# Sliding-window attention feeding a cosine MLP: where q, k and v are loaded and turned within a stage, and three normalisations on another engine

## The chip, the cores and the metric

The kernel runs on one core of a Trainium2 chip. The metric is device time in microseconds (us); the time before is 332.21 us, the median of three runs (330.58 to 332.81). Everything below is read from one profiled execution and its trace.

A core has five engines, each with its own queue that is worked off in order. TensorE (PE) multiplies; its weight loads are shown as PEld. VectorE (DVE) and ScalarE (ACT) read TensorE's results out of PSUM and work on them. GpSimd (POOL) cannot read PSUM; here it normalises, copies, and issues the loads of q, k and v, which are converted from 32 to 16 bit on their way. SyncE (SP) issues the DMAs that transpose, and the stores. SP's and POOL's transfers have a queue each (q1 and q0 on the page), and the same 16 DMA engines serve both.

## The reference, cut to what matters

```python
# q, k, v: (8, 8, 576, 64)   batch, heads, positions, head size
scores = (q @ k^T) / 8
keep   = 0 <= pos_q - pos_k < 64            # causal window of 64
attn   = softmax(where(keep, scores, -1e9)) @ v
x = attn.transpose(0, 2, 1, 3).reshape(8 * 576, 8 * 64)     # 4608 x 512
h = x @ w_in                                # 512 x 2048
out = (h * cos(h)) @ w_out                  # 2048 x 512
```

A block of 64 queries needs its own 64 keys and the 64 before them, so a *unit* is 64 queries by 128 keys of one batch, one pair of heads (128 rows of q, two heads) and one block j of 0 to 8.

## The kernel before, in words

**Stages.** The 4608 rows of x are worked off in nine tiles of 512 rows, mt = 0 to 8 (L485). A stage is one tile through the MLP: 64 matmuls with w_in (L359, into `h_ps`), with sine on ScalarE (L504) and the product on VectorE (L507) behind them, and then 64 matmuls with w_out (L519, into `out_ps`). Eight blocks make a tile and nine make a batch, so tile mt needs the last blocks of batch mt - 1 and the first ones of batch mt; of batch mt it needs blocks 0 to 5 in tile 2, 0 to 4 in tile 3, and 0 to 3, 0 to 2, 0 and 1 after that.

**Attention inside a stage.** Beside stage mt the attention of batch mt + 1 is computed, in groups of three or four units (`groups`, cut up by `CUTS`, L29). Each group passes through `g_scores` (PE, L263), `g_max` (DVE, L286), `g_exp` (ACT, L297), `g_inv` (DVE, L304), `g_norm` (POOL, L311; tile `w`), and `g_trans`: a DMA transpose that SP issues (L323; tile `wT`). In the first stage some groups (`direct`) are transposed on PE instead. `values` (PE, L338) multiplies wT by v into `o_ps`; `put_x` (L112) copies that into `xT`, the next tile's operand. PE works in the order in which it was given its work: the scores of the groups stand between the out_ps matmuls, from the first of them on, and `values` stands at the end of the stage, ahead of the next stage's h_ps matmuls. A stage has ten groups; the first four to seven of them (six in stages 1 and 2, four in stages 3 to 6) hold the blocks that the next tile needs.

**Loads and turns.** For a batch b from 2 on, `load_chunk` (L146) loads q and k in five chunks each, `load_v` (L152) loads v in five, all from POOL's queue. `turn` (L213) transposes a whole q or k in two DMAs from SP's queue, a main one (16 blocks of 128 by 128) and a small one; the results are `qX` and `kX`. `spread_q` (DVE, L221) copies qX into the block layout `qB` that the scores use; `spread_v` (POOL, two copies at L112) writes the copies of v that are shifted by 64 rows.

**The plan.** `at(time, fn, ...)` puts a step into a list with a time in units of about one us of a stage (a stage has T = 32 units), and `pump(time)`, called after each of the stage's steps, emits all steps that are due. So the planned times settle the order in each engine's queue, and nothing else: no instruction waits for a time. For batch b, t0 = 32 (b - 1) is the start of stage b - 1, in which its scores are computed (from t0 + 14.6 units on).

Before, in a stage from 2 to 5, POOL's queue holds, after the last normalisation of a stage: k (5 loads), q (5), then v (5), then the next stage's first five or six normalisations, `spread_v`, and the rest. SP's queue holds two stores, kX, qX, then the ten `wT`. k and q that are loaded in a stage are those of the batch whose scores come one stage later; v is that of the scores at hand.

The tiles k, q, kX, qX, and v have two buffers each. A DMA's issue waits, in its engine's queue, for its data, for its buffer, and for the DMA eight before it on the same engine to have landed.

Of the kernel before, what the change touches and what calls it, by code (L numbers as in the profile page):

```python
# [24 lines left out]
NC = 5  # L25
# [15 lines left out]
T = 2 * Q  # L41
# [17 lines left out]
def kernel(  # L59
# [182 lines left out]
    n_first = len(groups)  # L242
# [143 lines left out]
    def at(time, fn, *args):  # L386
        plan.append((time, len(plan), fn, args))
# [9 lines left out]
    n = n_first  # L397
    for t in range(B - 1):
        last = max(i for i, units in enumerate(groups) if units[0][0] == t + 1)
        time = T * t + Q - 1.4  # L400
        for i in range(last + 1 - n):
            time += PACE * len(groups[n - 1]) if i else 0
            at(time - 1.05 * (i % 2) * (t == 0), g_scores, n, i % 3)
            lags = LAGS[:2] + tuple(T * t + T - 0.79 - time + 0.01 * s for s in range(3)) if n == last and t else LAGS
            for lag, fn in zip(lags, (g_max, g_exp, g_inv, g_norm)):
                at(time + lag, fn, n)
            at(time + (4.6 if n in direct else lags[-1]), g_trans, n)
            if n in direct:
                at(time + 4.9, g_put, n)
            ready.update({unit: time + (5.9 if n in direct else 8.5) for unit in groups[n]})  # L410
            n += 1

    for b in range(1, B):
        t0 = T * (b - 1)
        if b == 1:
            for p in range(PAIRS):
                for lag, fn in ((0, tr_q), (0.01, tr_k), (0.02, put_q), (0.03, put_k)):
                    at(7 + 1.8 * p + lag, fn, b, p)
        else:
            for i, name in enumerate(("k", "q")):  # L420
                for c in range(NC):
                    at(t0 - T + 0.4 + 0.9 * (c + NC * i) if b > 2 else 4 + 0.5 * c if i else 27.5 + 0.9 * c, load_chunk, name, b, c)
                for c, (lo, hi) in enumerate(((0, 4), (4, 5))):
                    at((t0 + 3 if b == 2 and not i else t0 - T + 13.3 + 1.2 * i + (b == 2) * 9) + 0.6 * c, turn, name, b, lo, hi)
            for c, (lo, hi) in enumerate(((0, 4), (4, 5))):
                for h in range(2):
                    at(t0 + 4.2 + h + 2 * c, spread_q, b, h, lo, hi)
            for c in range(5):
                at(t0 + 9.4 + 0.9 * c, load_v, b, c)
            for half in range(2):  # L430
                at(t0 + 24.2 + 0.1 * half, spread_v, b, half)
    for half in range(2):
# [3 lines left out]
    for mt in range(1, n_mt):  # L436
        for p in range(PAIRS):
            time = max(ready[b, p - p % 2 + i // TU, j] for i in range(2 * TU) for b, j in (divmod(mt * TU + i % TU, NU),))
            time = max(time, 25.5) if mt == 1 else T * mt - (8.01 if mt == n_mt - 1 else 1.01)
# [27 lines left out]
    turn, turn_h = iter(range(100)), iter(range(100))  # L467
# [91 lines left out]
```

## Time and profile before

| What | Value |
|---|---|
| median of three runs | 332.21 us (330.58 to 332.81) |
| profiled execution, its own time | 332.94 us |
| its span | 331.2 us |
| mean granted TensorE clock | 0.968 |
| PE busy | 304.9 us, 92% of the span |
| ACT, DVE, POOL busy | 71%, 67%, 60% |
| DMA: q0 (POOL's loads), q1 (SP's) | 74.7% and 41.0% of 16 engines' span |
| h_ps matmuls, L359 | 576, 133.3 us |
| out_ps matmuls, L519 | 560, 132.8 us |
| normalisations on POOL, L311 | 78, 73.4 us, 956 ns in the mean |

Times are from the span's start. An entry such as `[3.36 <-DMA wT<-w]` behind a row is the idle time of the engine before it and what ended it. "SPq" rows are SP's issues of DMAs: their length is the time that the issue took SP's queue, not that of the transfer. "Landing" is the time from an issue's start to the moment at which the data are there.

The first scores of stages 1 to 6 start at 82.82, 119.88, 152.36, 184.48, 223.09 and 254.05 us. The later text calls these moments s1 to s6.

### The profile page before, as it was taken

To read this page: it belongs to the slowest core of one execution; us is meant where nothing else is said; L and a number is where in the kernel's file an instruction comes from. 1 tells how busy PE (TensorE), PEld (TensorE's weight loads), DVE (VectorE), ACT (ScalarE), POOL (GpSimd) and SP (SyncE) were. 2 spreads that over 40 slices of the span, in tenths; PEclk is the share of its full clock that TensorE was granted. 3 is DMA by queue.
4 is the path that set the end of the run, shared out by engine and by line. 5 is a ranking of instruction groups with operands and counts; after the bars stand their busy time and mean duration, and the time that the engine had idled before them with its cause. 6 is when DMAs were issued, how large, how long until landed. Compare 5 with 4: busy or idle time off the path is not lost.

```text
span 331.2 us, 7510 instructions
## 1 busy us (share of the span) xinstructions
PE 304.9 (92%) x2452; PEld 154.2 (47%) x2452; DVE 222.0 (67%) x847; ACT 236.0 (71%) x785; POOL 197.2 (60%) x218
## 2 busy tenths in 40 slices
PE   3989999589996999899999993999999999999996
PEld 2654554234543455445544551445544554454443
DVE  5896877449862887588749871598679857533811
ACT  3987799436992789778977895369977997314700
POOL 9995166999489627994699559843970690000000
PEclk9979999979996999999999998799999999999999
DMA  7999993999999999599979997999697435011012
GB/s 98 174 210 208 198 166 78 129 127 218 173 143 100 208 156 127 91 202 161 149 110 125 201 168 110 121 225 152 120 112 169 50 64 162 0 65 64 0 55 74
DMA packets 165960, 43.56 MB, mean 132 GB/s; under 512 B 155104, under 2 KB 161440, under 8 KB 165920
## 3 DMA queue, kind: packets, MB, share of 16 engines
q0 software_dynamic: 99632, 18.36, 74.7%
q1 hardware_dynamic: 66144, 24.52, 41.0%
q8 instruction: 19, 0.31, 0.4%
q14 instruction: 21, 0.17, 0.3%
q10 hardware_dynamic: 144, 0.20, 0.2%
HBM read 36.70 MB, written 9.44 MB: 139 GB/s over the span
## 4 chain that ended last, share of the span: by engine, by line
PE 53%; DMA 18%; POOL 11%; DVE 7%; issue 5%; ACT 3%; SPq 2%; POOLq 0%; DVEq 0%
PE h_ps L359 27%; PE out_ps L519 19%; DMA q<-in_q_dram 7%; DMA wT<-w 6%; POOL w L311 4%; DMA v<-in_v_dram 3%; POOL k L146 3%; DVE gT L507 3%; POOL v L112 2%; SPq L213 2%; ACT e L297 2%; PE o_ps L338 2%; PE s_ps L272 1%; DMA k<-in_k_dram 1%; PE s_ps L263 1%
## 5 line engine op out<-in xcount | busy, mean ns | idle before, releaser
L359 PE MATMUL h_ps<-xT,w_in 128*128 128x512 bf16 x576 | 133.3, 392 | 0.8 <-ACT xT L112 0.6
L519 PE MATMUL out_ps<-w_out,gT 128*128 128x512 bf16 x560 | 132.8, 379 | 0.0
L504 ACT ACTIVATE sin<-h_ps 128x512 f32<-128x512 f32 x144 | 83.2, 598 | 53.5 <-PE h_ps L359 52.2
L507 DVE TENSOR_TENSOR gT<-h_ps,sin 128x512 bf16<-128x512 f32 x144 | 93.6, 687 | 34.9 <-ACT sin L504 34.1
L311 POOL TENSOR_TENSOR w<-e,rden 128x512 bf16<-128x512 f32 (+1 forms) x78 | 73.4, 956 | 45.9 <-DVE rden L304 44.0
L297 ACT ACTIVATE e<-s,negm 128x128 f32<-128x128 f32 x256 | 98.6, 388 | 0.0
L359 PEld LDWEIGHTS <-w_in 128*128 128x128 bf16 x576 | 56.9, 101 | 70.2 <-issue 8.7
L519 PEld LDWEIGHTS <-gT 128*128 128x128 bf16 x560 | 51.5, 98 | 49.9
L286 DVE CUSTOM_DVE_ANT_0 s<-s_ps,mask 128x128 f32<-128x128 f32 x256 | 58.7, 286 | 1.7 <-PE s_ps L272 1.6
L297 ACT ACTIVATION_READ_ACCUMULATOR e<-s,negm 128x1 f32 x256 | 48.2, 188 | 0.0
L152 POOL DMA_DIRECT2D v<-in_v_dram x40 | 35.1, 888 | 15.3 <-PE h_ps L359 5.2
L112 DVE CAST xT<-o_ps 128x512 bf16<-128x512 f32 x27 | 17.9, 684 | 26.6 <-PE o_ps L338 26.5
L146 POOL DMA_DIRECT2D q<-in_q_dram x30 | 26.7, 922 | 9.5 <-DMA w_out<-in_moe_w_out_dram 9.2
L112 ACT COPY out_sb<-out_ps 128x512 f32<-128x512 f32 (+1 forms) x18 | 10.2, 566 | 28.1 <-PE out_ps L519 22.6
L338 PE MATMUL o_ps<-wT,v 128*64 128x64 bf16 x576 | 15.1, 204 | 15.1 <-DMA wT<-w 14.8
L304 DVE RECIPROCAL rden<-den 128x4 f32<-128x4 f32 (+1 forms) x80 | 13.9, 173 | 21.2 <-ACT e L297 20.3
L146 POOL DMA_DIRECT2D k<-in_k_dram x30 | 25.7, 872 | 0.0
L112 POOL COPY v<-v 64x2048 bf16<-64x2048 bf16 (+1 forms) x13 | 22.4, 1720 | 4.0 <-DMA v<-in_v_dram 3.6
L263 PEld LDWEIGHTS <-qB 128*128 128x128 bf16 x216 | 17.1, 98 | 14.2
L338 PEld LDWEIGHTS <-v 128*64 128x64 bf16 x576 | 12.4, 118 | 20.5 <-issue 19.8
L263 PE MATMUL s_ps<-kX,qB 128*128 128x128 bf16 x216 | 21.8, 219 | 0.0
L286 DVE DVE_READ_ACCUMULATOR2_ANT negm<- 128x1 f32 x256 | 21.2, 83 | 0.0
(53 smaller groups left out, 167.9 us busy)
## 6 DMA issues: line engine op xcount, KB each, us to landing
out_dram<-out_sb SPq DMA_DIRECT2D x16, 512.0 KB, 7.3
v<-in_v_dram POOLq DMA_DIRECT2D x32, 128.0 KB, 11.4
q<-in_q_dram POOLq DMA_DIRECT2D x24, 128.0 KB, 9.8
k<-in_k_dram POOLq DMA_DIRECT2D x24, 128.0 KB, 6.1
w_out<-in_moe_w_out_dram POOLq DMA_DIRECT2D x2, 1024.0 KB, 16.5
w_in<-in_moe_w_in_dram POOLq DMA_DIRECT2D x2, 768.0 KB, 12.1
wT<-w SPq DMA_TRANSPOSE x66, 3.4
out_dram<-out_sb SPq DMA_DIRECT2D x3, 256.0 KB, 2.0
```

What stands on the lines that cost most here:

```text
L112: {"a": nc.scalar.copy, "p": nc.gpsimd.tensor_copy}.get(engine, nc.vector.tensor_copy)(out, in_)
L146: nc.gpsimd.dma_start(out=st[name, b][:n, c].rearrange("p (h d) -> p h d", h=H), in_=src.rearrange("h p d -> p h d"))
L152: nc.gpsimd.dma_start(out=vt.rearrange("p (h d) -> p h d", h=H), in_=v[b, :, c * 128:c * 128 + n, :].rearrange("h p d -> p h d"))
L263: nc.tensor.matmul(out=s_ps[:, u].rearrange("p (a t) -> p a t", a=2), lhsT=q_block(b, p, j), rhs=k_blocks(b, p, j), start=True, stop=True, ...
L286: nc.vector.tensor_tensor_reduce(out=s[:, u], in0=s_ps[:, u], in1=mask[:, 2 - j % 2 if j else 0], scale=-scale if b else -1.0, scalar=BIG, ...
L297: nc.scalar.activation(e[:, u], s[:, u], AF.Exp, bias=negm[:, u:u + 1], scale=1.0 if n < n_first else -1.0, accum_out=den[:, u:u + 1])
L311: (nc.gpsimd if engine == "p" else nc.vector).tensor_tensor(out=w[:, 0:u], in0=e[:, 0:u], op=ALU.mult, in1=rden[:, 0:u].unsqueeze(2).to_br ...
L338: nc.tensor.matmul(out=o_ps[64 * h:64 * h + 64, 64 * i:64 * i + 64], lhsT=vtiles[b % 2][:, max(j - 1, 0), 128 * p + 64 * h:128 * p + 64 * ...
L359: nc.tensor.matmul(out=st["h", ff], lhsT=w_in_sb[:, ks, ff * 128:ff * 128 + 128], rhs=st["xT", mt][:, ks], start=start, stop=stop)
L504: nc.scalar.activation(sin, h_ps, AF.Sin, bias=math.pi / 2.0)
L507: nc.vector.tensor_tensor(out=gt[:, e], in0=h_ps, in1=sin, op=ALU.mult)
L519: nc.tensor.matmul(out=o_ps[e], lhsT=gT[ff // 2][:, ff % 2, ms * 128:ms * 128 + 128], rhs=w_out_sb[:, ff], start=ff == 0, stop=ff == n_ff - 1)
```

## The change

- `load_chunk` and `load_v`: a stage's loads now go v (t0 + 0.4 units), then the next batch's q and k (4.9 units and on). For batch 2, k's loads follow q's at once, in stage 0.
- `turn` of q: from 14.5 units into the stage to 26.2 (t0 - 5.8), which is behind the first six or seven weight groups of that stage in SP's queue. For batch 2 it is ahead of them, at 18.6.
- `turn` of k: from 13.3 units into the stage before to t0 + 0.2, the start of the stage that uses it; in SP's queue behind all ten weight groups of the stage before, and ahead of that stage's two stores.
- The normalisations of the first three groups of batch 1 (stage 0) go from POOL to DVE.

In SP's queue, from stage 3 on, this makes: six wT, qX (2 DMAs), four wT, kX (2 DMAs), two stores. In POOL's, behind the last normalisation: five v, five q, five k. The first scores of a stage, which PE reaches right behind the last h_ps matmul, now wait for the main kX DMA issued in the same stage.

```diff
             for lag, fn in zip(lags, (g_max, g_exp, g_inv, g_norm)):
-                at(time + lag, fn, n)
+                at(time + lag, fn, n, *("d" for _ in range(1) if fn is g_norm and n < n_first + 3))
...
-            for i, name in enumerate(("k", "q")):
+            for i, name in enumerate(("q", "k")):
                 for c in range(NC):
-                    at(t0 - T + 0.4 + 0.9 * (c + NC * i) if b > 2 else 4 + 0.5 * c if i else 27.5 + 0.9 * c, load_chunk, name, b, c)
+                    at(4 + 0.5 * (c + NC * i) if b == 2 else t0 - T + 4.9 + 0.9 * (c + NC * i), load_chunk, name, b, c)
                 for c, (lo, hi) in enumerate(((0, 4), (4, 5))):
-                    at((t0 + 3 if b == 2 and not i else t0 - T + 13.3 + 1.2 * i + (b == 2) * 9) + 0.6 * c, turn, name, b, lo, hi)
+                    at((t0 + 0.2 if i else 18.6 if b == 2 else t0 - 5.8) + 0.1 * c, turn, name, b, lo, hi)
...
             for c in range(5):
-                at(t0 + 9.4 + 0.9 * c, load_v, b, c)
+                at(t0 + 0.4 + 0.9 * c, load_v, b, c)
```

## The prediction

> **What bounds the kernel now.** I began with the page's engine shares: PE is busy 92% of the span, so the gain that is to be had is PE's idle time and its slow time. PE's waits come next, then the chain for the longest of them, the timelines of PE, SP and POOL around it, and the granted clock by stretches. The first row is from PE's waits, the next six from the chain in order of time, the rest from PE's timeline and the stretches.
>
> ```profile
> PE o_ps L338 <- DMA wT<-w: 14.8, 8, 3.4
> ...
> 179.76 12.95 DMA q<-in_q_dram
> 192.73 5.14 SPq L213
> ...
> 197.97 1.20 SPq L213
> ...
> 199.26 2.46 DMA wT<-w
> ...
> 201.88 4.93 DMA wT<-w
> ...
> 206.86 0.88 PE o_ps L338 x20
> ```
>
> ```profile
> 207.67 15.58 PE L359 MATMUL h_ps<-xT,w_in 128*128 128x512 bf16 x64
> ...
> 240.24 13.97 PE L359 MATMUL h_ps<-xT,w_in 128*128 128x512 bf16 x64
> ```
>
> ```profile
> 98.30:101.70 3.40, 1.61 (x47) 0.97 (x46) 0.95 (x3) 3.38 (x10) 3.40 (x5) 1.00 0.54 109
> 101.70:105.10 3.40, 2.12 (x24) 1.19 (x24) 1.29 (x2) 0.01 (x1) 3.40 (x5) 0.50 0.91 92
> 105.10:108.50 3.40, 3.40 (x10) 1.21 (x8) 0.00 (x0) 0.36 (x1) 3.40 (x5) 0.50 2.87 84
> ...
> 135.80:139.20 3.40, 1.98 (x69) 1.50 (x69) 1.59 (x4) 2.96 (x7) 3.40 (x4) 1.00 0.53 96
> ```
>
> `values` waits for weights, 14.8 us in eight waits: 4.8 before 67.6, 2.95 before 102.98, 1.4, 0.4, and 5.2 before 206.86. The chain says why: SP's queue holds the turn of q ahead of the ten wT, and that turn stood waiting for q's load until 192.73. Each long gap costs a second time. The stretches (PE busy first, granted clock third from last) show the clock at 0.50 for 3.4 or 6.8 us after a stretch of 3.4 us in which PE was busy 1.61 us or less, and not after 1.98 us. So 64 h_ps matmuls took 15.58 us after the gap at 206.86, and 13.97 after none. The three half-clock phases (67.6, 101.7, 204.1) cost 1.5 + 2.4 + 1.6 = 5.5 us. A stage without gap or half clock is 240.24 to 271.20, 31.0 us. All that can be won is thus 14.8 + 5.5 = 20.3 us.
>
> **What the change wins.** In stages 2 to 5 the first weight groups no longer stand behind a turn. The fourth normalisation ends 10 us after the scores begin (231.93 + 1.04 against 223.09), its wT needs 1.2 us of issue and 2.4 to 3.4 to land, and `values` begins 15.9 us after the scores: the waits at 138, 170 and 201 to 207 go. Tile 2's does not quite, since it needs the sixth group, normalised behind `spread_v` (97.66 + 1.04 = 98.70, `values` at 98.73): some 2 us stay. In stage 0, qX goes ahead of the wT, but beside k's loads, which POOL now issues at about 45.6 to 50. q's last load landed at 50.4; a main turn beside loads held SP for 4.8 to 6.3 us in four cases, so the first wT is issued near 57.5 instead of 53.45 and the four land from about 60 to 64; PE wants them from 59.7 on. Of the 4.8 us about 1.5 stay. The three normalisations on DVE are two of 128x512 (1.29 and 1.35 us in the first stage's two) and one of 128x384, some 3.6 us between 46 and 54 us, where DVE idles under 2 us; PE's transposes and ACT's exponents wait for it, about 1.2 us. Start of stage 1: -4.8 - 1.5 (half clock) + 1.5 + 1.2 = -3.6 us (bounds -6.3 and 0).
>
> **What it pays: the turn of k.** The scores of a stage stand in PE's queue right behind the h_ps matmuls, 31.0 us after the scores of the stage before if nothing waits, and now need a kX that is issued in the same stage. I follow SP from one stage's scores, s, to that landing, with these rows of POOL and SP (the third is the only qX issued while no load ran; the last lines are the landings of kX's first main DMA, and of the last wT before 212.9):
>
> ```profile
> 237.34 4.39 POOL L311 TENSOR_TENSOR w<-e,rden 128x384 bf16<-128x384 f32 x5
> ```
>
> ```profile
> 55.01 3.35 SPq L213 DMA_TRANSPOSE qX<-q  x2
> ...
> 93.18 13.23 SPq L323 DMA_TRANSPOSE wT<-w  x10
> ```
>
> ```profile
> DMA to landing us min/median/max: 9.5/9.5/9.5
> ```
>
> ```profile
> DMA to landing us min/median/max: 7.5/7.5/7.5
> ```
>
> 1. The sixth normalisation stands behind the five first and `spread_v`'s 3.4 us: it ends at 237.34 + 0.83 = s + 15.1 (s = 223.09).
> 2. Its wT: 13.23 / 10 = 1.3 us of SP's queue. s + 16.4.
> 3. qX, both DMAs, beside no loads (the stage's own have landed by then): 3.4. s + 19.8.
> 4. Four wT: 5.3. kX is issued at s + 25.1.
> 5. Landing. The six main kX of before took 9.5, 12.7, 10.9, 9.8, 11.9 and 12.3 us. Five had two stores just ahead of them; the first, 9.5, had none, and loads beside it. Here POOL issues v, q and k from s + 18.6 on (241.68 - 223.09), so the turn has loads beside it for its whole length, and four wT ahead that take 5 to 7.5 us to land beside loads. The ends: 4.3, a qX beside nothing, and 12.7. I take 10.5, between the 9.5 and the median of 11.4. kX is there at s + 35.6.
>
> PE wants it at s + 31.0 and so stands still for 4.6 us, with the out_ps matmuls queued behind the scores. Such a gap leaves some 3.4 us stretch with PE busy under 1.6 us, so by the rows above the clock halves. It then falls on the out_ps matmuls between the first groups' scores (eight, 1.73 us, become 3.5), and the chain through ACT and POOL to step 1 starts about 1.5 us later in the next stage.
>
> The five intervals between first scores, before: 37.1, 32.5, 32.1, 38.6, 31.0, in sum 171.2 (82.82 to 254.05). After:
> - s1 to s2: the sixth group ends at s + 15.9; 15.9 + 1.3 + 3.4 + 5.3 + 10.5 = 36.4.
> - s2 to s3: seven wT ahead of qX, three behind; 15.9 + 1.3 + 3.4 + 4.0 + 10.5 + 1.5 = 36.6.
> - s3 to s4, s4 to s5: 35.6 + 1.5 = 37.1 each.
> - s5 to s6: stage 6 loads v alone, five chunks, landed after 9 us (241.68 to 250.8), so kX lands about when PE is there: 31.0 + 2.1 for the half clock = 33.1.
>
> Sum 180.3, or 9.1 us more. After s6 nothing waits, before or after. In all -3.6 + 9.1 = +5.5 us on the profiled execution's 332.9 (span 331.2 and 1.7 around it), 338.4. That execution lies 0.7 above the median of 332.2, so I say **338 us**.
>
> What I cost at nothing: loading v first (`spread_v` waits for v in four of the stages now, 1.2 and 2.4 us at most, and POOL's later groups no longer need it soon); the two stores behind kX (each output buffer is wanted 4 us after the scores, the stores land some 3 and 5 us after kX; if that cover goes, DVE's copy waits and the groups with it, 1 to 2 us a stage); POOL's issues (15 loads took 16.3 us, 205.52 to 221.8, and end at s + 35, before the next normalisation at s + 31 + 4.2 or later).
>
> The Trainium skill (TensorE: Matmul & The Clock Gate, Part 1: The HAM clock gate) has the clock halve after a whole idle window of about 3.4 us, free-running. The trace disagrees: the stretch ahead of 101.7 held 1.6 us of matmuls and was followed by half clock. By the page's rule, an estimate, a gap of 4.6 us would hold a whole window in about one case in three, and the sum would be nearer 335.
>
> **Rivals.**
> *A, the turn is in time (faster).* kX lands in 7.4 us, as the main qX at 192.73 did beside v's last loads and behind nothing. Then s + 25.1 + 7.4 = 32.5, a gap of 1.5 us that leaves the clock alone: 33.3 + 32.0 + 32.5 + 32.5 + 31.0 = 161.3, 9.9 less, in all -13.5: 319 us. For it: the stores no longer stand ahead. Against: wT beside loads do, and loads have only begun. It decides below a landing of about 8.5 us.
> *B, the gap without its tail.* Landing 9.5, and the half clock is made up by ACT's slack: 35.4 + 34.1 + 34.6 + 34.6 + 32.0 = 170.7, as before; -4 in all: 329 us. For it: the first kX; against: ACT is busy without a pause in that phase (4.00 of 4 us from 124 on).
> *C, worse.* Landing at 12.3, as the last kX, and the stores hold up DVE: 1.8 more in four intervals and 1.5 more in two: 348 us.
>
> **Chances.** Forecast 0.42, A 0.27, B 0.18, C 0.13. Faster by over 1% is A, 0.27; B counts as within 1%, 0.18; slower is the forecast and C, 0.55. One per cent, 3.3 us, is about what a measurement of this kernel can tell from no change. The range, 319 to 348, goes from A to C; the forecast's own is 334 to 343.
>
> **What would show it.** In the profile after: PE's wait of scores at L263 for `kX`, four of them at 3 to 6 us, none at s6 over 2; the waits of `values` for wT gone but for about 3 us; four half-clock phases that start at scores and none at `values`; kX issued about 25 us after the scores, landing 9.5 to 12 later; s1 near 79. I am wrong if kX lands in 8 us (the DMA engines serve a lone turn faster than I take from turns behind stores), if PE waits for qB instead, or if the direct groups on DVE hold up stage 0 by more than the 3.6 us.

## The result and the profile after

| | Before | After |
|---|---|---|
| median | 332.5 us (330.6 to 335.5) | 350.3 us (347.5 to 351.5) |
| profiled execution, its own time | 332.9 us | 350.5 us |
| its span | 331.2 us | 348.7 us |
| mean granted clock | 0.968 | 0.961 |

The changed kernel takes 1.0515 times as long, with an interval of 1.0414 to 1.0617. The forecast was 338 us with a range of 319 to 348. The direction was right and the size was not: +5.5 us was forecast, and the span grew by 17.5. 350.3 lies above the range.

First the page of the changed kernel: the engines' shares, the chain that ended last by line, and the group of the scores (busy us, mean ns, then the idle time before it).

```profile
PE 306.8 (88%) x2452; PEld 153.7 (44%) x2452; DVE 225.2 (65%) x850; ACT 238.0 (68%) x785; POOL 194.1 (56%) x215
...
PE out_ps L519 22%; PE h_ps L359 17%; DMA kX<-k 11%; POOL w L311 5%; DMA v<-in_v_dram 4%; POOL v L112 4%; DVE gT L507 2%; PE s_ps L263 2%; ACT e L297 2%; POOL v L152 2%; DVE s L286 1%; DMA k<-in_k_dram 1%; DMA wT<-w 1%; PE o_ps L338 1%; POOL q L146 1%
...
L263 PE MATMUL s_ps<-kX,qB 128*128 128x128 bf16 x216 | 23.1, 228 | 27.6 <-DMA kX<-k 27.6
```

PE's share fell from 92% to 88%, and k's turn now makes up 11% of the chain. PE's waits in the changed kernel (us in total, times, the longest) say how often:

```profile
PE s_ps L263 <- DMA kX<-k: 27.6, 4, 8.0
...
PE o_ps L338 <- DMA wT<-w: 2.5, 2, 1.6
```

So the change did what it says on its winning side: the waits of `values` for weights went from 14.8 us to 2.5. It paid 27.6 us for that, in four waits of the first scores for kX. The chain from SP to PE can be followed in stage 2 (s2 = 117.58, s3 = 157.80). SP's timeline of the changed kernel, start and length of each row:

```profile
135.75 3.56 SPq L213 DMA_TRANSPOSE qX<-q  x2
139.42 4.05 SPq L323 DMA_TRANSPOSE wT<-w  x3
143.65 9.04 SPq L213 DMA_TRANSPOSE kX<-k  x2
152.79 1.06 SPq L382 DMA_DIRECT2D out_dram<-out_sb  x2
```

The main one of those two kX, in the answer for that tile:

```profile
L213 SPq DMA_TRANSPOSE kX<-k x1: 7717/7717/7717, 143.7 to 143.7; - x1
...
DMA to landing us min/median/max: 14.1/14.1/14.1
```

It is issued 26.1 us after s2, lands 14.1 us later, at 157.75, and 0.05 us after that PE begins the scores. PE's timeline of the changed kernel there:

```profile
147.71 2.37 PE L359 MATMUL h_ps<-xT,w_in 128*128 128x512 bf16 x10
157.80 0.61 PE L263 MATMUL s_ps<-kX,qB 128*128 128x128 bf16 x4 [7.72 <-DMA kX<-k]
158.20 3.42 PE L519 MATMUL out_ps<-w_out,gT 128*128 128x512 bf16 x8
...
163.85 1.89 PE L519 MATMUL out_ps<-w_out,gT 128*128 128x512 bf16 x8
```

The gap is 7.72 us. Behind it eight out_ps matmuls take 3.42 us, and 1.89 us a little later: the half clock. The granted clock by stretches of 3.4 us (third column from the right; PE busy is the first behind the length) shows it beginning inside the gap and ending 3.4 us into the work:

```profile
154.40:157.80 3.40, 0.00 (x0) 0.01 (x1) 0.00 (x0) 0.00 (x0) 0.00 (x0) 0.51 2.00 154
157.80:161.20 3.40, 3.40 (x12) 1.47 (x13) 0.93 (x8) 1.65 (x8) 0.00 (x0) 0.50 1.24 324
161.20:164.60 3.40, 3.40 (x26) 1.98 (x25) 2.66 (x20) 2.33 (x13) 1.04 (x1) 0.99 1.29 85
```

What the DMA engines did while that kX was on its way, in 40 slices (busy share in tenths, GB/s) and by queue (packets, MB, share of 16 engines; q0 is POOL's loads, q1 is SP's):

```profile
DMA  9999999999109999999999999999999999999999
GB/s 169 141 138 139 154 162 174 150 93 14 8 9 96 141 161 149 152 154 153 153 129 147 159 160 159 159 158 158 158 158 161 159 158 158 154 144 154 154 149 146
...
q0 software_dynamic: 8335, 1.05, 168.4%
q1 hardware_dynamic: 3689, 0.91, 53.1%
```

All engines are busy in all but two slices, at 140 to 160 GB/s together for most of the time, and more of the packets are POOL's than SP's. Eight of the 15 loads of the stage had been issued when the turn was, and one had landed. This view is the heart of the case. It also has a standstill: in three slices, about 3.2 to 4.4 us behind the issue, the engines move 8 to 14 GB/s; the last section comes back to it.

The forecast's steps against the profile, interval by interval:

| Interval | forecast | measured | kX issued after s: forecast, measured | landing: forecast, measured |
|---|---|---|---|---|
| s1 to s2 | 36.4 | 38.1 | 25.9, 26.6 | 10.5, 11.4 |
| s2 to s3 | 36.6 | 40.2 | 26.1, 26.1 | 10.5, 14.1 |
| s3 to s4 | 37.1 | 40.9 | 26.6, 27.0 | 10.5, 13.8 |
| s4 to s5 | 37.1 | 39.5 | 26.6, 27.7 | 10.5, 11.8 |
| s5 to s6 | 33.1 | 33.4 | | |
| sum | 180.3 | 192.1 | +2.2 in all | +9.1 in all |

The start of stage 1 is 3.3 us earlier (79.50 against 82.82; forecast 3.6), the intervals are 20.9 longer (192.1 against 171.2), and the rest after s6 is the same (77.1): -3.32 + 20.85 = 17.5, which is the span's growth.

### The profile page after: what moved, and what is told of

Same layout as the page of the kernel before. It is cut to its first block, busy times and chain, and to the rows that moved or that the text cites. A ratio compares the mean times of both kernels' runs of the same rounds, so it can differ in the third digit from the quotient of the medians.

```text
span 348.7 us, 7499 instructions
## 1 busy us (share of the span) xinstructions
PE 306.8 (88%) x2452; PEld 153.7 (44%) x2452; DVE 225.2 (65%) x850; ACT 238.0 (68%) x785; POOL 194.1 (56%) x215
## 4 chain that ended last, share of the span: by engine, by line
PE 46%; DMA 18%; POOL 15%; DVE 9%; issue 8%; ACT 3%; POOLq 0%; SPq 0%; DVEq 0%
PE out_ps L519 22%; PE h_ps L359 17%; DMA kX<-k 11%; POOL w L311 5%; DMA v<-in_v_dram 4%; POOL v L112 4%; DVE gT L507 2%; PE s_ps L263 2%; ACT e L297 2%; POOL v L152 2%; DVE s L286 1%; DMA k<-in_k_dram 1%; DMA wT<-w 1%; PE o_ps L338 1%; POOL q L146 1%
## 5 line engine op out<-in xcount | busy, mean ns | idle before, releaser
L519 PE MATMUL out_ps<-w_out,gT 128*128 128x512 bf16 x560 | 139.2, 392 | 0.0
L359 PE MATMUL h_ps<-xT,w_in 128*128 128x512 bf16 x576 | 129.2, 382 | 1.5 <-DVE xT L112 0.6
L311 POOL TENSOR_TENSOR w<-e,rden 128x512 bf16<-128x512 f32 (+1 forms) x75 | 70.4, 955 | 76.6 <-DVE rden L304 73.2
L507 DVE TENSOR_TENSOR gT<-h_ps,sin 128x512 bf16<-128x512 f32 x144 | 93.3, 690 | 26.6 <-ACT sin L504 26.2
L359 PEld LDWEIGHTS <-w_in 128*128 128x128 bf16 x576 | 55.8, 98 | 67.6 <-issue 3.5
L519 PEld LDWEIGHTS <-gT 128*128 128x128 bf16 x560 | 53.2, 101 | 53.5 <-issue 6.3
L263 PE MATMUL s_ps<-kX,qB 128*128 128x128 bf16 x216 | 23.1, 228 | 27.6 <-DMA kX<-k 27.6
L152 POOL DMA_DIRECT2D v<-in_v_dram x40 | 34.1, 871 | 3.5 <-DMA k<-in_k_dram 1.9
L146 POOL DMA_DIRECT2D q<-in_q_dram x30 | 27.9, 956 | 9.1 <-PE h_ps L359 4.6
L304 DVE RECIPROCAL rden<-den 128x4 f32<-128x4 f32 (+1 forms) x80 | 13.8, 172 | 11.1 <-ACT e L297 10.4
L112 DVE COPY out_sb<-out_ps 128x512 f32<-128x512 f32 x18 | 12.4, 690 | 13.1 <-PE out_ps L519 13.0
L221 DVE COPY qB<-qX 64x2048 bf16<-64x2048 bf16 (+1 forms) x24 | 16.4, 685 | 0.4
## 6 DMA issues: line engine op xcount, KB each, us to landing
w_in<-in_moe_w_in_dram POOLq DMA_DIRECT2D x2, 768.0 KB, 12.7
```

The costliest lines, as they stand in the source:

```text
L112: {"a": nc.scalar.copy, "p": nc.gpsimd.tensor_copy}.get(engine, nc.vector.tensor_copy)(out, in_)
L146: nc.gpsimd.dma_start(out=st[name, b][:n, c].rearrange("p (h d) -> p h d", h=H), in_=src.rearrange("h p d -> p h d"))
L152: nc.gpsimd.dma_start(out=vt.rearrange("p (h d) -> p h d", h=H), in_=v[b, :, c * 128:c * 128 + n, :].rearrange("h p d -> p h d"))
L221: nc.vector.tensor_copy(to.rearrange("d (m i) t -> d m i t", i=n), of[d, lo:hi, :, 0:64 * n].rearrange("d c a (i t) -> d (c a) i t", i=n))
L263: nc.tensor.matmul(out=s_ps[:, u].rearrange("p (a t) -> p a t", a=2), lhsT=q_block(b, p, j), rhs=k_blocks(b, p, j), start=True, stop=True, ...
L311: (nc.gpsimd if engine == "p" else nc.vector).tensor_tensor(out=w[:, 0:u], in0=e[:, 0:u], op=ALU.mult, in1=rden[:, 0:u].unsqueeze(2).to_br ...
```

## The experiments

All changes are to the changed kernel unless another is named. The ratios are to the kernel before, measured beside each.

### k's turn right behind q's

```diff
-    at((t0 + 0.2 if i else 18.6 if b == 2 else t0 - 5.8) + 0.1 * c, turn, name, b, lo, hi)
+    at((t0 + (0.2 if b == 2 else -5.6) if i else 18.6 if b == 2 else t0 - 5.8) + 0.1 * c, turn, name, b, lo, hi)
```

> The changed kernel with one edit undone in part: from batch 3 on, k's turn stands right behind q's (one weight group between them at most), ahead of the last weight groups of the stage, and not at the start of the next one. Theory (the late turn of k costs it all): kX is issued about 20 us after a stage's scores, before the next loads begin, lands in 4 to 8 us, well ahead of the next scores at 31 us; the four waits of scores for kX (27.6 us) and the half-clock phases at scores go, and nothing takes their place: intervals between first scores of 31 us but for one of 33, about 316 us in all. Rival (SP's queue and the transfers are full, so the wait only moves): the last weight groups of a stage or the store come late instead, waits of values or of DVE appear, and the time is 325 to 335 us.

Measured: 328.5 us, ratio 0.9956 (0.9909 to 1.0003); the profiled execution, 332.0, was the longest of its ten. Most of the loss is gone, and no gain is left. kX is issued 21 to 25 us after the scores, some 4 earlier, but still lands 10.6 to 12.3 us later wherever the next batch's q and k load beside it. PE's waits in this kernel:

```profile
PE s_ps L263 <- DMA kX<-k: 8.9, 3, 3.8
...
PE o_ps L338 <- DMA wT<-w: 2.8, 3, 1.6
PE s_ps L263 <- DVE negm L286: 1.9, 3, 1.1
```

and one of DVE's, from the same kernel:

```profile
DVE out_sb L112 <- DMA out_dram<-out_sb: 8.6, 3, 3.3
```

The wait moved in part, as the rival had it, and a new one came. The two stores, which now go behind the last weight groups beside the loads, land so late (119.49 in stage 2, where DVE wants the buffer at 116.2) that DVE's copies of out_ps wait for their buffers, 8.6 us in three waits. The scores' maxima stand behind those copies. Rival C of the forecast had expected this of the stores in the changed kernel. In the changed kernel itself DVE has no such wait: there the stores of stage 2 land at 160.2 and 161.8, but the scores begin only at 157.8, kept back by kX.

### No loads of q and k beside the turn

```diff
 def load_chunk(name, b, c):
+    if b > 3:
+        st[name, b] = st[name, b - 2]
+        return
```

This leaves out the loads of q and k for batches 4 to 7, so those batches compute with the tiles of two batches before. All turns, stores and loads of v stay.

> The changed kernel without the loads of q and k for batches 4 to 7: these batches are computed from the q and k of two batches before (part of the computation is left out), all turns stand where the change put them. Theory (the landing is long because the turn shares the DMA engines with loads): kX is issued 25 to 26 us after the scores as in the changed kernel, lands in about 5 us as it did in stage 6 (4.8), and PE waits at no scores for more than 1 us: about 315 to 318 us. Rival (the place in SP's queue is late enough by itself): kX still lands 10 us or more after its issue, waits of 4 us and more stay at the scores, 340 to 350 us.

Measured: 314.9 us, ratio 0.9478 (0.9426 to 0.9531), with SP's queue in the changed order. kX is issued 25.0 to 26.9 us after the scores, as in the changed kernel, and lands 4.3 to 6.3 us later instead of 11.4 to 14.1. PE's waits:

```profile
PE o_ps L341 <- DMA wT<-w: 2.3, 2, 1.6
...
PE s_ps L266 <- DMA kX<-k: 0.6, 1, 0.6
```

The intervals are 32.6, 31.7, 31.0, 31.2 and 31.0, and no half clock is left. So the place of k's turn in SP's queue is affordable by itself: without those loads the loss is gone. Leaving them out also takes their issues off GpSimd and their traffic away from wT and the stores, so this run alone does not say that it is the turn that they slow. The last experiment, with all loads in place, bears on that.

### The stage-0 parts alone, in the kernel before

```diff
-                at(time + lag, fn, n)
+                at(time + lag, fn, n, *("d" for _ in range(1) if fn is g_norm and n < n_first + 3))
...
-    at(t0 - T + 0.4 + 0.9 * (c + NC * i) if b > 2 else 4 + 0.5 * c if i else 27.5 + 0.9 * c, load_chunk, name, b, c)
+    at(t0 - T + 0.4 + 0.9 * (c + NC * i) if b > 2 else 4 + 0.5 * c + 2.5 * (1 - i), load_chunk, name, b, c)
...
-    at((t0 + 3 if b == 2 and not i else t0 - T + 13.3 + 1.2 * i + (b == 2) * 9) + 0.6 * c, turn, name, b, lo, hi)
+    at((18.6 if i else t0 + 0.2) + 0.1 * c if b == 2 else t0 - T + 13.3 + 1.2 * i + 0.6 * c, turn, name, b, lo, hi)
```

> The kernel before with the part of the change for stage 0 and 1 alone: k of batch 2 is loaded right behind q, q's turn of batch 2 stands ahead of the weight groups, k's at the start of stage 1, and three normalisations are on VectorE; from batch 3 on all as before. Theory: the first scores of stage 1 start at 79.5 us, as in the changed kernel, 3.3 us earlier than before, and the rest is unchanged: 329 us. Rival (the 3.3 us are lost again to a later wait, since k and q of batch 3 are loaded earlier by no more than POOL's queue lets them): 332 us, within 1 us of the kernel before.

Measured: 330.1 us, ratio 0.9935 (0.9904 to 0.9967). s1 comes at 80.26, 2.6 us earlier than before, and the intervals are those of before (171.0 in sum). The part of the change that concerns stage 0 and batch 2 is a gain of some 2 us, and separate from the rest.

### The gap filled with matmuls

```diff
+    def fill(n):
+        o_ps = ps_t.tile([128, MT], F32, tag="t", name="fill_ps")
+        for i in range(n):
+            nc.tensor.matmul(out=o_ps, lhsT=w_in_sb[:, 0, 0:128], rhs=w_out_sb[:, 0], start=i == 0, stop=i == n - 1)
...
+            if i == 0 and 2 <= t <= 5:
+                at(time, fill, 22)
```

The 22 matmuls stand ahead of the first scores of stages 2 to 5, where PE would wait anyway; their results are never read. They keep the clock whole.

> The changed kernel with 22 more matmuls of 128x512 in front of the first scores of stages 2 to 5 (results never read), 4.8 us at full clock, less than the waits there (5.3 to 8.0 us), so that PE works where it stood still. Theory (the clock halves because of the gap and slows the chain from scores to the sixth normalisation by 0.5 to 2.1 us): the clock stays at 1.0 there, that normalisation ends 15 to 16 us after the scores instead of 16.4 to 17.2, the four intervals after these scores shrink by 5.4 us in all, about 345 us. Rival (the slower clock lies beside the chain through ScalarE and GpSimd, and costs nothing): 350 us as it is.

Measured: 342.0 us, ratio 1.0296 (1.0224 to 1.0367), some 8 us faster than without the matmuls. No half clock is left at the scores, and the sum of the intervals falls by 10.2 us, to 181.9. That is more than the half clock was priced at in the forecast (1.5 us in each of three intervals and 2.1 in the last, 6.6 in sum) and than the 5.4 expected here, and part of it is shorter landings. So I ran both kernels again, side by side, and a third for the loads.

### Both again, and one without k's loads

The first is the changed kernel unaltered and the second the one with the 22 matmuls. The third leaves out only k's loads of batches 4 to 7, which then compute with the k of two batches before:

```diff
 def load_chunk(name, b, c):
+    if b > 3 and name == "k":
+        st[name, b] = st[name, b - 2]
+        return
```

> The changed kernel itself, a second time, to see which of its numbers repeat. Its first profile had main kX landings of 11.4, 14.1, 13.8 and 11.8 us and intervals in sum 192.1. Theory: the landing beside loads is a fixed price for this order of transfers, so all four repeat within 1 us, the time within 347 to 352. Rival: between 11 and 14 us it is scatter from how the packets of the two queues fall; then the four come in another order, the mean between 11 and 13, and the time may lie 3 us lower.

> The kernel with 22 extra matmuls ahead of the first scores of stages 2 to 5, a second time and beside the changed kernel on one chip. The first time it was 8 us faster, and in the profile 4 us of that were later issues of kX and 5 us longer landings. Theory: only the half clock is cured, which moves the start of the next stage's work by about 1.5 us in three stages and 2 in the last: 6.5 us between the two kernels, landings in the mean within 0.7 us of those of the changed kernel beside it. Rival: the landings are really shorter with the clock whole, by 1 to 2 us in stages 3 and 4: 8 to 11 us between the two.

> The changed kernel without k's loads for batches 4 to 7 (the k of the batch two before is turned again); v's and q's loads and the order of all turns stay. Theory: the turn shares the DMA engines with whatever is loaded at the same time, so a third of the loads less shortens its landing by about that part of the 8 us that loads add: 8.5 to 10.5 us in place of 12.8, waits of 2 to 4 us at the scores, 326 to 338 us. Rival 1: what is left of v's and q's loads still covers the whole turn, and the landing stays at 11 to 13 us: 344 to 351 us. Rival 2: it is k's loads alone, last in the queue and the ones that run beside the turn's end, that stretch it: landing 5 to 7 us, no wait, 315 to 320 us.

| | median | ratio to before | main kX landings, stages 1 to 4 | half clock at scores |
|---|---|---|---|---|
| changed, first | 350.3 | 1.0515 (1.0414 to 1.0617) | 11.4, 14.1, 13.8, 11.8 | 4 phases |
| changed, again | 351.0 | 1.0557 (1.0528 to 1.0587) | 11.9, 13.9, 13.4, 11.9 | 4 phases |
| gap filled, first | 342.0 | 1.0296 (1.0224 to 1.0367) | 11.7, 12.0, 10.9, 11.6 | none |
| gap filled, again | 342.2 | 1.0288 (1.0230 to 1.0347) | 11.7, 11.6, 10.8, 11.9 | none |
| no k loads | 347.6 | 1.0489 (1.0429 to 1.0548) | 9.4, 14.0, 12.3, 10.2 | 3 phases |

Three things follow. The landings are a price and not scatter: they repeat within 0.5 us, stage by stage. The gap's filling is worth 8.9 us (351.0 - 342.2) in time and 10.5 in the second pair's intervals, 192.8 against 182.3. Of these, 5.6 are kX's earlier issue (0.7, 1.4 and 1.8 in stages 2 to 4) and the last interval (1.7), close to the 6.6 of the forecast. Another 4.8 are the landings of stages 2 and 3 (2.3 and 2.5); the rival had the time, and expected the shorter landings in stages 3 and 4. And a third of the loads less did little: 11.5 us in the mean against 12.8, so the theory (8.5 to 10.5) fell and the first rival held. In stage 2 of that kernel the DMA engines look just as before while kX is on its way:

```profile
DMA  9999999999013999999999999999999999999439
GB/s 152 154 158 153 151 158 160 217 156 60 5 9 26 155 153 135 145 148 152 155 147 120 159 158 159 158 158 159 158 159 159 159 159 153 166 247 180 32 108 385
...
q0 software_dynamic: 6688, 0.84, 117.5%
```

k's loads are the last in POOL's queue. Without them the engines are still full, from v's and q's loads, until shortly before the turn has landed. Only the first and last of the four landings became shorter by more than 1.5 us against the changed kernel beside it. I read from this that what has already been issued when the turn is issued decides more than what is issued behind it, but no run tests that alone. With k's turn right behind q's only 3 to 6 loads had been issued and it still took 10.6 to 12.3 us; with 1 or 2, in the last experiment, 6.4 to 8.9.

### The loads in the order of before

```diff
-    at(4 + 0.5 * (c + NC * i) if b == 2 else t0 - T + 4.9 + 0.9 * (c + NC * i), load_chunk, name, b, c)
+    at(4 + 0.5 * (c + NC * i) if b == 2 else t0 - T + 0.4 + 0.9 * (c + NC * (1 - i)), load_chunk, name, b, c)
...
-    at(t0 + 0.4 + 0.9 * c, load_v, b, c)
+    at(t0 + 9.4 + 0.9 * c, load_v, b, c)
```

> The changed kernel with the loads in the order of the kernel before (k, q, then v) and the turns as changed, so SyncE's queue is the same. Theory: any load beside k's turn lengthens it alike, whichever tensor it brings, and nothing waits soon for v; the order of the loads is worth nothing: within 3 us of the changed kernel, 346 to 353 us, landings of kX 11 to 14 us. Rival 1: v first is what keeps the shifted copies of v out of GpSimd's way; with v last, spread_v waits for v's last load in stages 2 to 5 and the later groups come 1 to 3 us later each: 352 to 360 us. Rival 2: v's loads are the ones that collide (their chunks go to another layout): kX lands in 9 to 10 us, 338 to 342 us.

Measured: 347.8 us, ratio 1.0482 (1.0424 to 1.0540); kX lands after 10.8, 12.8, 13.6 and 11.0 us, and PE waits for it 24.4 us in four waits. That is some 3 us less than with v first, and the time is inside the theory's band: the order of the loads is not what costs.

### k's turn while GpSimd copies the shifted v

Between the fifth and the sixth weight group of a stage, SP has nothing to do for 2.8 to 3.3 us (in stage 2 for 1.5, ahead of the seventh), because POOL is at `spread_v`; and no load has started.

```diff
-    at((t0 + 0.2 if i else 18.6 if b == 2 else t0 - 5.8) + 0.1 * c, turn, name, b, lo, hi)
+    at((t0 + (0.2 if b == 2 else -7.3) if i else 18.6 if b == 2 else t0 - 5.8) + 0.1 * c, turn, name, b, lo, hi)
```

> The changed kernel with one edit: for batches from 3 on, k's turn is issued ahead of the sixth weight group (stage 2: the seventh), while GpSimd copies the shifted v, instead of behind all ten groups. The loads stay where the change put them. Theory: what k's turn costs is that it runs beside the loads; before the loads of a stage start (some 20 us after the scores) the DMA engines are quiet. Then kX is issued about 12 us after the scores and lands in 4.3 to 5 us, as the turns without any load beside them did; no wait at the first scores, no half clock, the waits of values for wT at most 3 us in all; intervals 32.6, 31.5, 31.3, 31.3, 31 us, the whole 313 to 318 us. Rival 1: SyncE's queue is the limit; the turn makes the sixth weight group and q's turn late, the last four groups then fall beside the loads and values waits 1 to 3 us a stage: 322 to 328 us. Rival 2: with k's turn gone from behind the groups the two stores go beside the loads and hold up VectorE's copies, as behind q's turn: 324 to 330 us.

Measured: 326.6 us, ratio 0.9834 (0.9775 to 0.9893). That is 1.7% faster than before, with an interval clear of no change, but slower than the theory said. kX is indeed issued some 13 us after the scores and no score waits for it. PE waits elsewhere:

```profile
PE h_ps L359 <- DVE gT L507: 6.5, 8, 3.6
...
PE o_ps L338 <- DMA wT<-w: 4.4, 3, 3.2
```

DVE's timeline says why PE's h_ps matmuls waited for `gT`:

```profile
144.21 0.69 DVE L221 COPY qB<-qX 64x2048 bf16<-64x2048 bf16 x1 [5.22 <-DMA qX<-q]
144.82 0.68 DVE L507 TENSOR_TENSOR gT<-h_ps,sin 128x512 bf16<-128x512 f32 x1
```

Now q's turn was the one in the loads. It was issued 19.8 us after the scores and took 9.3 to land, and the copy of qX into qB, which stands ahead of the products in DVE's queue, held them up for 5.2 us. In stage 1 the sixth group's wT stood behind kX and `values` waited 3.2 us for it. The first rival's place (SP's queue makes q's turn late) was right, and its time, 322 to 328, too.

### The same with the three normalisations on GpSimd

This is the kernel just shown, with one part of the change undone:

```diff
-    at(time + lag, fn, n, *("d" for _ in range(1) if fn is g_norm and n < n_first + 3))
+    at(time + lag, fn, n)
```

> The same as the kernel with k's turn while GpSimd copies the shifted v, but with the three normalisations of stage 0 back on GpSimd. Theory: GpSimd is issuing loads until about 50 us, so the first weight groups of stage 0 come some 2 to 4 us later and so does stage 1: 2 to 4 us slower than with them on VectorE. Rival: the first groups of stage 0 are transposed by TensorE and are not what the first stage waits for (that is q's and k's turn of batch 2 and the transposes behind it): within 1 us.

Measured: 328.7 us, ratio 0.9888 (0.9824 to 0.9952), 2.2 us slower than with them on VectorE. s1 comes at 81.52 instead of 79.17. PE's transposes wait for POOL's normalisation here for

```profile
PE tw_ps L320 <- POOL w L311: 6.0, 3, 3.3
```

against 1.7 us in the kernel it is compared with. The first of the three starts on GpSimd at 50.22 us, behind the last of k's loads, issued at 49.52; on VectorE it starts at 46.45. So that part of the change is worth about 2 us, by taking the first groups out from behind POOL's issues of loads.

### Both turns ahead of the loads

```diff
-    at((t0 + 0.2 if i else 18.6 if b == 2 else t0 - 5.8) + 0.1 * c, turn, name, b, lo, hi)
+    at((t0 + (0.2 if b == 2 else -8.8 if b == 3 else -5.8) if i else 18.6 if b == 2 else t0 - (5.8 if b == 3 else 7.3)) + 0.1 * c, turn, name, b, lo, hi)
```

> The changed kernel with both turns moved into SyncE's idle places before the loads start: in stage 1, k's turn goes ahead of the fifth weight group and q's stays behind the sixth; from stage 2 on, q's turn goes to where GpSimd copies the shifted v, and k's goes right behind the next weight group (the sixth, in stage 2 the seventh). Theory: with k's turn in q's way, q's turn was issued 18 to 20 us after the scores and landed 6 to 9 us later among the loads, and VectorE waited for qX with TensorE's h_ps matmuls behind it (3.6 and 1.2 us, and 3.2 us for the sixth weight group of stage 1, each with its half clock). Now qX lands about 18 us after the scores, kX is issued some 17 to 20 us after them and lands by 29, ahead of the 31 at which it is wanted. Intervals 32.7, 31.5, 31.2, 31.2, 31.0 us, in sum 157.6; span 314, time 313 to 318 us, ratio 0.945 to 0.957. Rival 1: k's turn now has the first loads beside it and lands 10 to 12 us after its issue; in stage 2 that is 31 to 33 us after the scores, a wait of 1 to 2 us there and none elsewhere: 316 to 321 us. Rival 2: the stores, issued among the loads, hold up VectorE's copies and with them the groups: 320 to 328 us.

Measured: 319.8 us, ratio 0.9631 (0.9583 to 0.9679), 3.7% faster than before and, by the two ratios, 8.4% faster than the changed kernel. The loads, the normalisations and the instructions are those of the changed kernel; only SP's order differs. SP's timeline in stage 3 of this kernel (s3 = 146.07):

```profile
159.76 4.35 SPq L213 DMA_TRANSPOSE qX<-q  x2
164.21 1.20 SPq L323 DMA_TRANSPOSE wT<-w  x1
165.63 4.35 SPq L213 DMA_TRANSPOSE kX<-k  x2
```

The DMA engines while that qX was on its way:

```profile
DMA  9999940000499800010999999999999999900038
GB/s 291 244 333 271 273 63 0 0 0 0 105 168 52 16 11 9 9 9 9 237 291 291 121 280 291 291 291 289 291 278 289 291 291 291 213 0 0 0 66 162
...
q1 hardware_dynamic: 2851, 0.71, 105.6%
```

This is a turn among no loads. The engines rest for over a quarter of the time, they move some 290 GB/s when they work, and the turn has landed in 4.5 us. kX of stages 2 to 5, issued 19.5 to 19.7 us after the scores and 0.1 to 0.9 us behind the first load of the stage, lands 6.4 to 8.9 later, ahead of the 31 us at which it is wanted. PE's longest waits are:

```profile
PE tq_ps L176 <- DMA q<-in_q_dram: 4.8, 1, 4.8
PE o_ps L338 <- DMA wT<-w: 4.3, 2, 3.4
```

The intervals are 36.1, 31.0, 31.5, 31.8 and 31.4. The expected 313 to 318 was missed by 2 us: the intervals' sum is 161.9 where 157.6 was expected, and 3.4 of the 4.3 are in the first. There `values` waited 3.45 us for the sixth weight group, whose wT landed at 99.2, and a half-clock phase from 99.5 followed. The time lies in the first rival's band (316 to 321) by luck, since none of the rivals had that wait: k's landing cost nothing, and the stores held DVE's copies up by 3.1 us in two waits of which PE's waits show 0.2.

## Why the prediction was wrong in size

**The start of stage 1: the number right (-3.6 forecast, -3.3 measured), by luck in its parts.** The waits of `values` there fell from 4.8 us to 0.9, more than the 3.3 that the forecast took off. The normalisations on DVE took 0.69, 0.69 and 0.56 us, 1.9 in place of 3.6, and behind them, at 59.4 us, PE was 0.64 us later than before (0.25 of it from ahead of them), not 1.2. Against that the half clock gave back little of its 1.5 us: the 61 h_ps matmuls ahead of s1 took 14.7 us with it before, and 14.4 without it after. What kept them there I did not find. The forecast also had the normalisations as a cost alone. With k's loads where the change puts them they are a gain of 2.2 us, as the kernel with them on GpSimd shows. The kernel with the stage-0 parts alone confirms the sum (2.6 us), not its terms.

**The waits of `values`, right.** 2.5 us are left, the "some 2 us" of tile 2 and 0.9 in stage 0.

**Steps 1 to 4, the issue of kX, right within 1.1 us.** 26.6, 26.1, 27.0 and 27.7 us after the scores, where the steps gave 25.9, 26.1, 26.6 and 26.6: 2.2 us in sum.

**Step 5, the landing, failed.** I took 10.5 us, between the 9.5 of the one turn without stores ahead and the median of before, 11.4, with 12.7 as the upper end. Measured were 11.4, 14.1, 13.8 and 11.8, two of them above that end. This step is 9.1 of the 11.8 us that were missing in the intervals. It has two parts. The first, some 4 us, is the credit that I gave for the stores: their absence ahead of the turn gained nothing here, since without half clock the four land in 11.7, 11.6, 10.8 and 11.9, about the median of before and 1.0 more than I took. I argued from what stands ahead in SP's own queue, where POOL's queue sets the landing: with SP's order kept and q's and k's loads gone it is 4.3 to 6.3 us, with the loads kept and the turn 4 us earlier still 10.6 to 12.3. The other 5 us are the longer landings of stages 2 and 3, which go when the gap is filled. How many loads run beside the turn does not explain them, for with k's loads gone stage 2 still took 14.0. Two things in the traces go with them, and the cause is open (below). The upper end of 12.7 came from six rows of one execution. In the kernel with the stage-0 parts alone, which has the order of before from batch 3 on, one of these turns took 13.65 where before it took 11.89.

The Trainium skill (DMA: Bandwidth & Descriptors, section "Issuing engines are not separate DMA queues") says that transfers started by different engines run on the same 16 DMA engines and interleave. The trace agrees as far as it goes, with 8335 packets of q0 and 3689 of q1 while one kX was on its way.

**The half clock, right in size.** Three intervals at 1.5 us and 2.1 in the last were forecast, 6.6; filling the gap gave back 5.6 in the issue and the last interval. The phases came where they were said to, at the scores of s2 to s5. Filling it also gave back 4.8 us of landing, which no step had, and the cause of that stays open (below).

**Costed at nothing.** v's loads first: right, within 3 us of the other order. The two stores behind kX: right in the changed kernel, as DVE has no wait for them; with kX earlier they cost DVE 8.6 us, so the cover was the lateness of everything else. POOL's issues: the issuing itself held nothing up in these stages; the loads that it started are what the turn paid for.

**The rivals.** A asked for a landing below 8.5 us and B for 9.5; neither came near. C had the landing nearest (12.3) and the time nearest (348), with the wrong second half: the stores did not hold DVE up. With the measured landings in the forecast's own sum, 338.4 + 9.1 = 347.5, C's time is reached without them.

## What to carry to other kernels

Price a moved transfer by rows in which the DMA engines carry the same company over its whole flight, whichever queue issues that, and give no credit for what no longer stands ahead of it in its own queue. Here such a turn took 4.5 us alone and 11 to 14 beside a stage's loads, and moving k's turn 6 to 9 us forward (15 in stage 1) and q's, from stage 2 on, by 4 to 5, to where the loads have not begun or only just, turned 5% slower into 3.7% faster.

## What the runs showed of the hardware that I had not expected

- **Two rates of the DMA engines.** Beside POOL's loads (126 bytes a packet: 1.05 MB in 8335) the 16 engines are busy nearly without a pause and move 140 to 160 GB/s in all; a turn alone (249 bytes a packet: 0.71 MB in 2851) moves 290. While that kX was on its way, SP's queue moved 0.91 MB in 14.1 us; with the turn among no loads, 0.71 MB in 4.5. I read this as the loads setting the pace for what runs beside them.
- **The half clock needs no empty stretch.** In the kernel with k's turn while GpSimd copies v, the clock halved at 144.1 behind this stretch with 1.24 us of matmuls:

```profile
140.70:144.10 3.40, 1.24 (x6) 0.49 (x5) 0.00 (x0) 0.74 (x2) 2.56 (x4) 1.00 2.28 151
144.10:147.50 3.40, 1.96 (x5) 0.69 (x5) 3.23 (x6) 0.65 (x2) 2.52 (x3) 0.50 1.90 136
```

  The Trainium skill (TensorE: Matmul & The Clock Gate, Part 1: The HAM clock gate) has it halve after an idle window of about 3.4 us. The trace disagrees here as it did before the change (1.61 us), and the measurement decides. In the changed kernel the two do not differ, as gaps of 5.3 to 8.0 us were followed by half clock each time. Gaps of 2.28 and 2.79 us, in the kernel with k's turn behind q's, left the clock whole; one of 3.80 us did not. How many microseconds of matmuls a stretch holds does not settle it either: the profile before put the line between 1.61 us (halved) and 1.98 (not), but a stretch with 1.31 (180.7 to 184.1 in that same kernel) and one with 1.51 (110.5 to 113.9 in the changed kernel's second profile) left the clock whole.
- **Shorter landings with the gap filled, unexplained.** In stages 2 and 3 the same transfers in the same order landed 2 to 3 us sooner in both profiles with the extra matmuls. It is not the half clock of that stage itself: in the kernel without k's loads no half clock came before 151.2, and its kX, issued at 140.1, still took 14.0 us. Two things in the traces go with the long landings.

  The first is the standstill of the DMA engines. The eight landings of stages 2 and 3 in the changed kernel (both profiles), without k's loads and with the loads in the order of before all have one, of 0.6 to 1.4 us under 40 GB/s. The four of the filled kernel have none; no slice of their views is under 130 GB/s. That is up to half of the difference.

  The second is the time from the issue of the stage's first load to that of the main kX. Over stages 1 to 4 of these six profiles, the nine turns issued 6.1 to 7.1 us behind that load landed in 12.0 to 14.1 us, and the fifteen issued 7.2 to 8.1 us behind it in 9.4 to 11.9. In the second pair, stage 2 has 6.5 us unfilled and 7.2 filled; the kernel without k's loads has 6.4 there. It does not go on downwards: at 2.0 to 4.5 us (k's turn right behind q's) the landings were 10.6 to 12.3, and at 0.1 to 0.9 (the last experiment) 6.4 to 8.9.

  No run changed either of the two alone, so they are companions of the long landings and not shown to be their cause.
